# Last stage of a fused attention and two-mixture kernel: query tiles of 128, one shared last tile, later masks and another written order

## The chip, the cores and the metric

The kernel runs as one program on one core of a Trainium2 chip. The metric is the device time of one launch in microseconds; the time before is the median of three runs. A profiled execution of the same program gives the rows of this document; in it times count from the first instruction of the span.

## The reference

Three blocks follow one another, for 4 batches of 576 tokens and a width of 512. The last one is the one that the change touches:

```python
def _moe2_ref(x, w_gate, wq, wk, wv, wo):        # x: 4 x 576 x 512, 4 experts of width 64
    logits = x @ w_gate
    topk = np.argpartition(-logits, 2, axis=-1)[..., :2]
    ...                                          # w: softmax over the two chosen logits
    for e in range(E):
        q, k, v = x @ wq[e], x @ wk[e], x @ wv[e]
        scores = scale * (q @ k.transpose(0, 2, 1))
        scores = np.where(causal, -1000000000.0, scores)
        scores = scores - scores.max(-1, keepdims=True)
        a = np.exp(scores)
        a /= a.sum(-1, keepdims=True) + 1e-09
        ye = a @ v @ wo[e]
        ...                                      # out += (chosen weight of e, or 0) * ye
```

Before it stand a local attention plus an attention over pooled tokens (8 heads), and a mixer with a token part and a channel part of 1536 hidden channels. Everything is float32, and the products are made with more than one pass.

## The kernel before

The program has four stretches: the local and pooled attention with the token mixer (an order written out by hand, `STEPS`), the channel mixer (from about 180 us on, TensorE products of 460 and 462 columns, laid out by the scheduler), and then the last stage, the gated experts, whose order is the written table `LAST` (line 88). `tc.manual_schedule()` takes the words of the table one after the other, so that each engine's queue holds its own instructions in the order of the table; engines run freely against each other and wait by semaphores. Everything outside of those two tables is placed by the scheduler.

A word is a step and its indices. Per batch b: `vh`/`vl` split x into a high and a low part (ScalarE, GpSimd; two sets for six of the eight chunks of two batches, so batch 1 starts while batch 0 is in use), `v` makes values and gate logits of one token tile (12 products), `vc` and `lc` copy them out, `g`, `ge`, `gr`, `gw` make the gate weights. Per unit u = 2 b + p (batch b, expert pair p): `pj` projects half of the tokens to keys (0, 1) or queries (2, 3) with 12 products, `ph` and `pl` split the result into high and low parts, one expert's low part going to the other 64 partitions; `dk` swaps halves of K by DMA on SP's queue; `s.t.e` scores query tile t of expert e against all keys up to its end (two products, against K and its swapped copy; four for the last tile, in a PSUM tile of two banks of which there is one); `m` adds the causal mask and takes the row maximum (VectorE), `e` the exponential with its row sum (ScalarE), `q` the reciprocal, `r` the normalisation times the gate weight (VectorE), `t` turns the tile chunk by chunk on TensorE, `c` copies the turned chunks to SBUF (ScalarE), `a` multiplies by the values for one half of the queries (both experts side by side in the array), `ah`, `al` split the result. Per pair of batches: `w` multiplies 128 tokens by the output weights (3 products per expert pair), `y` copies the 512 columns out (in the last five tiles 288 by ScalarE and then 224 by VectorE), `dy` stores them.

Tokens go in tiles of TQ = 116: four of 116 and one of 112. For expert e of a unit the last tile is a 112 x 576 piece of its own with its own exponential, normalisation, five transposes and three copies. PSUM has six banks under the tag `b1`, given out in turn, and one tile of two banks. The score tiles (`Pc`) and output tiles (`y`) share eight SBUF buffers.

The masks `caus` (causal, line 173) and `before` (rank order of equal logits, line 174) are made by GpSimd at the head of the program, lines 187 to 193.

Of the kernel before, what the change touches and what calls it, by code (L numbers as in the profile page):

```python
# [13 lines left out]
OP = mybir.AluOpType  # L14
# [5 lines left out]
TQ = 116  # L20
NT = 5
TS = [TQ, TQ, TQ, TQ, S - 4 * TQ]
# [66 lines left out]
    vh0.0 vh0.1 vl0.0 vh0.2 vl0.1 vh0.3 vl0.2 vl0.3 v0.3 pj0.0 vh1.0 pj0.1 pj0.3 pj0.2 vh1.1 ph0.0 ph0.1 lc0.3 pl0.0  # L89
    ph0.3 v0.2 vc0.3 pl0.1 vc0.2 v0.0 lc0.2 lc0.0 dk0.0 ph0.2 pl0.3 pj1.0 dk0.1 s0.3.1 s0.3.0 pl0.2 s0.1.0 m0.3.1  # L90
    m0.3.0 s0.4.0 m0.4.0 ph1.0 pl1.0 e0.3.0 dk1.0 v0.4 e0.3.1 q0.3 vc0.0 s0.4.1 s0.0.1 m0.4.1 e0.4.0 lc0.4 s0.2.0
    v0.1 m0.2.0 pj1.1 e0.4.1 m0.1.0 vc0.1 vc0.4 s0.0.0 q0.4 lc0.1 g0 m0.0.1 vl1.0 gr0 m0.0.0 ge0 ph1.1 pl1.1 pj1.2
    dk1.1 vl1.1 e0.0.0 e0.1.0 pj1.3 gw0 ph1.2 e0.0.1 r0.3.0 r0.3.1 r0.4.0 t0.4.0 vh1.2 pl1.2 ph1.3 t0.3.0 t0.3.1
    s0.2.1 t0.5.0 pl1.3 s0.1.1 s1.4.0 r0.4.1 e0.2.0 vh1.3 m0.2.1 q0.0 c0.4.0 c0.3.0 m0.1.1 t0.4.1 c0.3.1 m1.4.0
    r0.0.1 c0.5.0 s1.3.0 vl1.2 e0.2.1 t0.5.1 m1.3.0 c0.4.1 vl1.3 q0.2 pj2.1 e0.1.1 ph2.1 t0.0.1 e1.3.0 q0.1 r0.0.0
    v1.0 r0.2.0 s1.3.1 r0.1.1 pl2.1 s1.4.1 vc1.0 lc1.0 r0.1.0 r0.2.1 c0.5.1 t0.2.0 s1.2.1 m1.3.1 e1.4.0 c0.0.1
    t0.1.0 c0.1.0 m1.4.1 m1.2.1 c0.2.0 v1.2 s1.2.0 e1.3.1 t0.0.0 dk2.1 e1.4.1 vc1.2 t0.1.1 pj2.0 c0.1.1 c0.0.0 q1.3
    m1.2.0 t0.2.1 e1.2.0 ph2.0 lc1.2 s1.1.0 s1.1.1 q1.4 r1.3.0 m1.1.0 r1.4.0 pj2.3 s1.0.1 pl2.0 m1.1.1 c0.2.1 t1.4.0
    ph2.3 r1.3.1 t1.5.0 m1.0.1 e1.1.0 t1.3.0 c1.3.0 e1.2.1 v1.4 c1.5.0 dk2.0 pl2.3 s1.0.0 lc1.4 q1.2 r1.4.1 e1.1.1
    r1.2.0 c1.4.0 v1.1 vc1.1 v1.3 t1.5.1 vc1.4 m1.0.0 t1.4.1 s2.3.0 q1.1 vh2.0 r1.1.0 c1.5.1 e1.0.0 r1.2.1 lc1.1  # L100
    lc1.3 e1.0.1 vc1.3 t1.3.1 m2.3.0 t1.2.1 c1.3.1 pj2.2 e2.3.0 c1.4.1 s2.3.1 s2.4.0 c1.2.1 g1 a0.1 q1.0 ge1 r1.1.1
    m2.4.0 a0.0 s2.4.1 t1.2.0 ph2.2 pl2.2 m2.3.1 t1.1.0 ah0.1 vh2.1 r1.0.0 ah0.0 al0.1 m2.4.1 al0.0 s2.1.0 e2.4.0
    m2.1.0 c1.1.0 r1.0.1 e2.3.1 t1.1.1 gr1 c1.1.1 c1.2.0 pj3.0 e2.1.0 ph3.0 t1.0.0 e2.4.1 pl3.0 s2.2.1 t1.0.1 s2.1.1
    c1.0.1 a1.1 m2.1.1 q2.3 c1.0.0 e2.1.1 m2.2.1 gw1 s2.2.0 pj3.1 q2.4 r2.3.0 ph3.1 ah1.1 pj3.2 r2.4.0 pj3.3 m2.2.0
    e2.2.0 pl3.1 al1.1 r2.3.1 e2.2.1 ph3.2 t2.4.0 ph3.3 r2.4.1 c2.4.0 t2.5.0 w0.3.0 q2.2 dk3.0 pl3.2 vh2.2 c2.5.0
    a1.0 q2.1 t2.5.1 vl2.0 pl3.3 w0.3.1 t2.3.0 vl2.1 ah1.0 t2.4.1 y0.3 c2.4.1 vl2.2 r2.2.0 c2.5.1 c2.3.0 r2.2.1
    w0.1.0 t2.3.1 al1.0 w0.1.1 s2.0.0 w0.2.0 r2.1.0 dk3.1 m2.0.0 y0.1 t2.2.1 vh2.3 w0.2.1 t2.2.0 s2.0.1 c2.3.1 y0.2
    t2.1.0 c2.2.0 s3.4.0 w0.0.0 c2.1.0 c2.2.1 e2.0.0 dy0.3 m2.0.1 e2.0.1 r2.1.1 s3.3.1 t2.1.1 vl2.3 dy0.1 q2.0
    m3.3.1 dy0.2 w0.0.1 s3.3.0 r2.0.0 y0.0 s3.2.0 s3.0.0 t2.0.0 m3.3.0 r2.0.1 m3.2.0 v2.0 vh3.0 e3.3.0 c2.1.1 m3.4.0
    t2.0.1 s3.2.1 s3.4.1 m3.0.0 e3.3.1 vc2.0 pj4.0 c2.0.1 pj4.1 q3.3 c2.0.0 m3.2.1 r3.3.0 ph4.0 lc2.0 e3.2.0 pl4.0  # L110
    v2.4 ph4.1 e3.4.0 e3.0.0 r3.3.1 t3.3.1 s3.0.1 t3.3.0 pl4.1 e3.2.1 c3.3.1 dy0.0 c3.3.0 m3.4.1 lc2.4 s3.1.0 dk4.0
    q3.2 r3.2.0 m3.1.0 pj4.3 vc2.4 a2.1 dk4.1 e3.4.1 vh3.1 ph4.3 m3.0.1 q3.4 s3.1.1 ah2.1 v2.2 a2.0 al2.1 r3.4.1
    pl4.3 r3.2.1 vc2.2 lc2.2 e3.1.0 ah2.0 t3.2.0 c3.2.0 s4.4.0 r3.4.0 t3.5.1 m3.1.1 t3.4.0 c3.4.0 m4.4.0 t3.5.0
    pj4.2 e3.1.1 vl3.0 c3.5.0 al2.0 s4.3.0 t3.2.1 c3.5.1 e3.0.1 ph4.2 q3.0 c3.2.1 v2.1 q3.1 vc2.1 pl4.2 s4.0.1
    r3.0.1 m4.3.0 r3.1.0 e4.4.0 vl3.1 v2.3 lc2.1 r3.0.0 t3.0.0 t3.4.1 t3.1.0 lc2.3 m4.0.1 g2 s4.4.1 vc2.3 t3.0.1
    c3.1.0 r3.1.1 m4.4.1 s4.1.0 c3.0.0 gr2 t3.1.1 s4.3.1 c3.4.1 s4.0.0 pj5.2 c3.0.1 ge2 m4.1.0 c3.1.1 e4.4.1 m4.0.0
    s4.2.0 q4.4 gw2 a3.1 r4.4.0 e4.0.0 e4.3.0 r4.4.1 m4.3.1 pj5.1 ph5.2 ah3.1 ph5.1 t4.4.0 pl5.2 c4.4.0 e4.0.1
    e4.3.1 al3.1 m4.2.0 pl5.1 t4.5.1 q4.3 pj5.3 t4.4.1 t4.5.0 a3.0 c4.5.0 pj5.0 dk5.1 r4.3.0 ph5.3 q4.0 c4.5.1
    r4.0.1 ah3.0 pl5.3 r4.0.0 e4.1.0 s4.2.1 c4.4.1 s4.1.1 vh3.2 ph5.0 t4.3.0 r4.3.1 al3.0 m4.2.1 pl5.0 vl3.2 m4.1.1
# [18 lines left out]
    c7.0.0 q7.1 t7.0.1 r7.1.0 r7.2.1 t7.5.1 w1.2.1 t7.4.1 c7.0.1 y1.1 r7.2.0 y1.2 c7.5.1 a6.0 r7.1.1 t7.2.0 ah6.0  # L138
    t7.2.1 dy1.1 al6.0 t7.1.1 c7.4.1 c7.1.1 w1.3.0 dy1.2 w1.7.0 t7.1.0 c7.2.0 c7.2.1 a7.1 w1.3.1 ah7.1 y1.3 w1.8.0
    w1.4.0 al7.1 c7.1.0 dy1.0 dy1.3 a7.0 w1.7.1 ah7.0 y1.7 w1.8.1 w1.6.0 al7.0 w1.4.1 dy1.7 w1.6.1 w1.5.0 y1.8 dy1.8  # L140
    y1.4 dy1.4 y1.6 w1.5.1 y1.5 dy1.6 dy1.5
"""


# [919 lines left out]
```

## Time and profile before

| | |
|---|---|
| time, median of 3 runs | 644.37 us (643.84 to 645.01) |
| profiled execution | 644.59 us, span 642.5 us |
| TensorE busy | 618.0 us, 96%, 5196 products |
| VectorE busy | 443.6 us, 69%, 1083 instructions |
| ScalarE busy | 361.5 us, 56%, 1061 instructions |
| GpSimd busy | 149.5 us, 23%, 167 instructions |
| mean granted TensorE clock | 0.999 |

A busy TensorE is a union of records, and records of successive products overlap: what a product takes from the queue is read from the starts of successive ones. In the groups by line a row has the number of instructions after the x, then busy time in us and the mean of one in ns. `PE` is TensorE, `PEld` its weight loads, `DVE` VectorE, `ACT` ScalarE, `POOL` GpSimd, `SPq` SP's queue of DMA issues; the text in brackets is idle time of the engine before the instruction and what ended it.

### The profile page before, as it was taken

The numbers are of one execution on the slowest core, as the hardware profiler recorded it, in microseconds if no ns is written. First come the engines' busy times: TensorE is split into PE (matmuls) and PEld (weight loads), VectorE is DVE, ScalarE is ACT, GpSimd is POOL, SyncE is SP. The second block draws the span as 40 slices with busy tenths as digits, with TensorE's granted clock in tenths as the row PEclk, the third lists the DMA queues.
The fourth block names the chain that finished last, engine by engine and source line by source line (L and its number), as shares of the span: only waits on it lengthen the run. The fifth ranks groups of instructions, "written<-read, shape, count | busy, mean of one in ns | idle before, by whom it ended". The sixth has DMA issues, their size and how long they took to land.

```text
span 642.5 us, 13638 instructions
## 1 busy us (share of the span) xinstructions
PE 618.0 (96%) x5196; PEld 554.6 (86%) x5196; DVE 443.6 (69%) x1083; ACT 361.5 (56%) x1061; POOL 149.5 (23%) x167
## 2 busy tenths in 40 slices
PE   4789999999999999999999999999989999999997
PEld 3678889999988889998888889999989889989885
DVE  7999998779696876467644554443497766857871
ACT  4898977765464453343422332420488777777783
POOL 6878986522131120010000000310010020010000
PEclk9999999999999999999999999999999999999999
DMA  8879484013132220020200100000111121021103
GB/s 266 250 234 279 130 248 119 13 46 116 42 106 88 66 87 12 1 66 0 67 0 1 51 16 1 2 0 1 44 35 37 29 76 38 20 100 40 37 33 117
DMA packets 28945, 46.76 MB, mean 73 GB/s; under 512 B 3216, under 2 KB 16016, under 8 KB 28880
## 3 DMA queue, kind: packets, MB, share of 16 engines
q1 hardware_dynamic: 28880, 45.90, 23.8%
q8 instruction: 41, 0.67, 0.5%
q14 instruction: 24, 0.20, 0.1%
HBM read 36.45 MB, written 4.72 MB: 64 GB/s over the span
## 4 chain that ended last, share of the span: by engine, by line
PE 87%; DVE 9%; DMA 1%; issue 1%; ACT 1%; POOL 1%; SPq 0%; ACTq 0%; DVEq 0%; POOLq 0%
PE c L219 47%; PE proj L219 7%; PE vp L219 4%; PE wo L219 4%; PE pu L219 4%; PE o L962 4%; PE pt L939 3%; PE h L219 3%; PE s L900 2%; PE s L901 2%; DMA wt_raw<-in_wt_dram 1%; PE tx L556 1%; PE sd L444 1%; DVE nraw L403 1%; PE tl L486 1%
## 5 line engine op out<-in xcount | busy, mean ns | idle before, releaser
L219 PE MATMUL c<-hl,wch 128*128 128x460 f32 (+1 forms) x240 | 89.3, 372 | 0.0
L219 PE MATMUL c<-hh,wcl 128*128 128x460 f32 (+1 forms) x240 | 89.1, 371 | 0.0
L219 PE MATMUL c<-hh,wch 128*128 128x460 f32 (+1 forms) x240 | 89.1, 371 | 0.0
L219 PE MATMUL c<-ul,wch 128*128 128x460 f32 (+1 forms) x240 | 89.0, 371 | 0.0
L219 PE MATMUL c<-uh,wch 128*128 128x460 f32 (+1 forms) x240 | 89.0, 371 | 0.0
L219 PE MATMUL c<-uh,wcl 128*128 128x460 f32 (+1 forms) x240 | 88.9, 370 | 0.0
L199 ACT ACTIVATE hh<-c 128x460 fp32r<-128x460 f32 (+1 forms) x60 | 33.0, 549 | 84.9 <-PE c L219 84.6
L795 POOL TENSOR_TENSOR vlo<-u,vh 128x576 fp32r<-128x576 f32 x16 | 22.8, 1427 | 238.7 <-ACT vh L791 215.1
L208 DVE SCALAR_TENSOR_TENSOR hl<-c,hh 128x460 fp32r<-128x460 f32 (+1 forms) x60 | 38.0, 634 | 48.7 <-ACT hh L199 48.5
L281 POOL TENSOR_TENSOR wc_t<-wc_f,wc_t 128x512 int32<-128x512 int32 x24 | 32.5, 1358 | 150.7 <-ACT wc_t L270 122.3
L663 DVE TENSOR_TENSOR ul<-u,uh 128x460 fp32r<-128x460 f32 (+1 forms) x80 | 53.1, 677 | 9.7 <-ACT uh L657 9.7
L657 ACT ACTIVATE uh<-u 128x460 fp32r<-128x460 f32 (+1 forms) x80 | 45.4, 585 | 23.8 <-PE c L219 19.0
L917 ACT ACTIVATE Pc<-Pc,nm 116x116 f32<-116x116 f32 (+4 forms) x80 | 46.7, 586 | 8.7 <-DVE nm L910 6.8
L910 DVE CUSTOM_DVE_ANT_0 Pc<-s,caus 116x348 f32<-116x348 f32 (+4 forms) x80 | 40.0, 514 | 14.6 <-PE s L901 10.9
L219 PEld LDWEIGHTS c<-hh,wch 128*128 128x128 f32 x240 | 45.2, 188 | 5.2
L219 PEld LDWEIGHTS c<-hh,wcl 128*128 128x128 f32 x240 | 45.1, 188 | 5.2
L219 PEld LDWEIGHTS c<-uh,wcl 128*128 128x128 f32 x240 | 45.1, 188 | 5.1
L219 PEld LDWEIGHTS c<-uh,wch 128*128 128x128 f32 x240 | 45.1, 188 | 5.0
L219 PEld LDWEIGHTS c<-hl,wch 128*128 128x128 f32 x240 | 45.1, 188 | 4.9
L219 PEld LDWEIGHTS c<-ul,wch 128*128 128x128 f32 x240 | 45.1, 188 | 4.9
L939 PE MATMUL pt<-ident,Pc 116*116 116x116 f32 (+2 forms) x240 | 35.2, 263 | 2.9 <-DVE Pc L928 2.6
L928 DVE TENSOR_SCALAR Pc<-Pc,su,gw 116x464 f32<-116x464 f32 (+4 forms) x80 | 36.3, 478 | 0.7
(216 smaller groups left out, 1650.6 us busy)
## 6 DMA issues: line engine op xcount, KB each, us to landing
wc_raw<-in_wc_dram SPq DMA_DIRECT2D x24, 512.0 KB, 3.6
vz<-in_vw_dram SPq DMA_DIRECT2D x16, 320.0 KB, 5.3
qT<-in_qT_dram SPq DMA_DIRECT2D x16, 288.0 KB, 5.0
kT<-in_kT_dram SPq DMA_DIRECT2D x16, 288.0 KB, 5.3
vr<-in_vp_dram SPq DMA_DIRECT2D x32, 144.0 KB, 4.2
K<-K SPq DMA_DIRECT2D x64, 72.0 KB, 2.0
out_dram<-y SPq DMA_DIRECT2D x18, 256.0 KB, 2.0
wt_raw<-in_wt_dram SPq DMA_DIRECT2D x4, 288.0 KB, 3.5
```

The source lines that it names most:

```text
L199: nc.scalar.activation(hi, src, AF.Relu if relu else AF.Copy, **({"scale": scale} if scale else {}))
L208: nc.vector.scalar_tensor_tensor(lo, src, 0.0, h, op0=OP.max, op1=OP.subtract)
L219: mm(ps, a, c, start=first and i == 0, stop=last and i == n - 1)
L281: nc.gpsimd.tensor_tensor(t, r["f"], t, op=OP.add)
L657: nc.scalar.activation(hi, UA[:, c, blocks[k]], AF.Copy)
L663: nc.vector.tensor_tensor(lo, UA[:, c, blocks[k]], hi.bitcast(F32), op=OP.subtract)
L795: nc.gpsimd.tensor_tensor(lo, U[b][:, c], hi.bitcast(F32), op=OP.subtract)
L910: nc.vector.tensor_tensor_reduce(dst, r["s", t, e], mask, -1.0, 3.0e38, OP.add, OP.min, nm[:nq])
L917: nc.scalar.activation(P[:nq, :n], P[:nq, :n], AF.Exp, bias=r["nm", t, e][:nq], scale=-1.0, accum_out=r["su", t][:nq, e:e + 1])
L928: nc.vector.tensor_scalar(P[:nq, :n], P[:nq, :n], r["su", t][:nq, e:e + 1], BR[b]["w"][:nq, t, 2 * p + e:2 * p + e + 1], op0=OP.mult, op1= ...
L939: tp(pt[:TS[c], (c - c0) * TQ:(c - c0) * TQ + nq], P[:nq, c * TQ:c * TQ + TS[c]], ident[:nq, :nq])
L962: mm(o[64 * e:64 * e + 64, a - q0:q1 - q0], BR[b]["VV"][:TS[c], c, ec:ec + 64], PT[e][:TS[c], column(c, a):column(c, a) + q1 - a], start=( ...
```

## The change

- `TQ` is 128: four query tiles of 128 and a rest `T4` of 64 tokens. The same tiles cut the keys and values into chunks of 128 and one of 64.
- The last tile holds 64 queries of expert 0 in partitions 0 to 63 and the same queries of expert 1 in partitions 64 to 127, in one of two fixed tiles `P4` of 640 columns, of which the last 64 are zero. Its scores and maxima are made per expert (`s.4.e`, `m.4.e`); exponential, reciprocal, normalisation, five 128 x 128 transposes and three copies are made once for both. The gate weights get a second small tile `gw4` for it, by two VectorE copies per batch. PT of both experts is one tile.
- Values `VV` and logits `L` get fixed tiles, whose rows 64 to 127 of the last token tile are zeroed once. GpSimd no longer clears L per batch.
- GpSimd fills `caus` and `before` and the zero parts behind the low parts of batch 0, just ahead of the last stage's table, not at the head of the program; `before` moves to another SBUF pool.
- The output tile that the table's last `w` makes (rows of batches 2 and 3, tile 5) is made in two halves of 256 columns, in two PSUM banks: VectorE copies the first and ScalarE the second, and each is stored by its own DMA.
- `LAST` is another table: the same steps in another order, without the second expert's `e`, `r`, `t` and `c` of the last tile.

```diff
-TQ = 116
+TQ = 128
 NT = 5
-TS = [TQ, TQ, TQ, TQ, S - 4 * TQ]
+T4 = S - 4 * TQ
+TROWS = [TQ, TQ, TQ, TQ, T4]
...
-    vh0.0 vh0.1 vl0.0 vh0.2 vl0.1 vh0.3 vl0.2 vl0.3 v0.3 pj0.0 vh1.0 pj0.1 pj0.3 pj0.2 vh1.1 ph0.0 ph0.1 lc0.3 pl0.0
-    ph0.3 v0.2 vc0.3 pl0.1 vc0.2 v0.0 lc0.2 lc0.0 dk0.0 ph0.2 pl0.3 pj1.0 dk0.1 s0.3.1 s0.3.0 pl0.2 s0.1.0 m0.3.1
-    m0.3.0 s0.4.0 m0.4.0 ph1.0 pl1.0 e0.3.0 dk1.0 v0.4 e0.3.1 q0.3 vc0.0 s0.4.1 s0.0.1 m0.4.1 e0.4.0 lc0.4 s0.2.0
-    v0.1 m0.2.0 pj1.1 e0.4.1 m0.1.0 vc0.1 vc0.4 s0.0.0 q0.4 lc0.1 g0 m0.0.1 vl1.0 gr0 m0.0.0 ge0 ph1.1 pl1.1 pj1.2
-    dk1.1 vl1.1 e0.0.0 e0.1.0 pj1.3 gw0 ph1.2 e0.0.1 r0.3.0 r0.3.1 r0.4.0 t0.4.0 vh1.2 pl1.2 ph1.3 t0.3.0 t0.3.1
...
-    w1.4.0 al7.1 c7.1.0 dy1.0 dy1.3 a7.0 w1.7.1 ah7.0 y1.7 w1.8.1 w1.6.0 al7.0 w1.4.1 dy1.7 w1.6.1 w1.5.0 y1.8 dy1.8
-    y1.4 dy1.4 y1.6 w1.5.1 y1.5 dy1.6 dy1.5
+    vh0.0 vl0.0 vh0.1 vh0.2 vl0.1 vl0.2 vh0.3 vl0.3 pj0.1 vh1.0 v0.1 pj1.1 vh1.1 v0.2 pj0.0 lc0.1 ph0.1 pl0.1 vl1.0
+    ph1.1 ph0.0 vc0.1 pl1.1 vc0.2 v0.0 pl0.0 pj0.3 pj1.0 ph1.0 lc0.0 lc0.2 pl1.0 ph0.3 pj0.2 ph0.2 vc0.0 v0.4 v0.3
+    pl0.2 dk0.1 lc0.4 pj1.2 dk0.0 pl0.3 vc0.4 lc0.3 s0.3.0 vc0.3 pj1.3 ph1.2 s0.3.1 s0.4.0 s0.1.1 vh1.2 g0 s0.1.0
+    gr0 vl1.1 m0.3.0 dk1.1 dk1.0 pl1.2 vl1.2 s0.2.0 ph1.3 s0.2.1 m0.3.1 m0.4.0 pl1.3 s0.4.1 vh1.3 m0.1.1 ge0 e0.3.0
+    s0.0.1 e0.3.1 s0.0.0 m0.1.0 m0.0.1 vh2.0 vl1.3 e0.1.0 m0.2.0 m0.2.1 gw0 q0.3 m0.4.1 s1.3.0 e0.1.1 v1.2 vc1.2
+    v1.0 e0.4 lc1.2 e0.2.0 pj2.1 e0.2.1 r0.3.0 ph2.1 lc1.0 r0.3.1 t0.3.0 vc1.0 s1.4.0 m0.0.0 pj2.0 q0.4 m1.3.0 q0.1
...
+    dy1.0 dy1.1 ah7.1 y1.3 al7.1 dy1.2 w1.8.0 dy1.3 w1.6.1 w1.7.1 w1.4.0 y1.6 y1.7 dy1.6 w1.8.1 dy1.7 y1.8 dy1.8
+    w1.4.1 w1.5.0 y1.4 w1.5.1 dy1.4 y1.5 dy1.5
...
+            r["w4"] = py.tile([TQ, 2], F32, tag="gw4", bufs=2, name="gw4")
+            for e in range(2):
+                es = slice(T4 * e, T4 * e + T4)
+                nc.vector.tensor_copy(r["w4"][es], r["w"][:T4, 4, e::2])
...
+            ps = b2("s")
+            r["s", t, e] = ps[:, :, :HS]
+            for h in range(2):
+                for i, K in enumerate((K1, K2)):
+                    mm(ps[:T4, h, :HS], Q[e][:, 4 * TQ:], K[e][:, h * HS:h * HS + HS], start=i == 0, stop=i == 1)
...
+            P, xs = P4[u % len(P4)], slice(T4 * e, T4 * e + T4)
+            r["P", t, None] = P
+            dst, mask = (y.rearrange("p (s n) -> p s n", s=2) for y in (P[xs, :S], caus[:T4, :S]))
+            nc.vector.tensor_tensor_reduce(dst, r["s", t, e][:T4], mask, -1.0, 3.0e38, OP.add, OP.min, nm[xs])
...
+        def turn(g, e=None):
+            t, cs = (g, range(g + 1)) if g < 4 else (4, range(4)) if g == 4 else (4, range(4, 5))
             pt = r["pt", g, e] = b1("pt")
+            for c in cs:
+                tp(pt[:, (c - cs[0]) * TQ:(c - cs[0]) * TQ + TQ], r["P", t, e][:, c * TQ:c * TQ + TQ], ident)
...
+            v = pt.rearrange("p (c e q) -> p e c q", e=2, q=T4)
+            if g == 4:
+                nc.scalar.activation(PT.rearrange("p e (c q) -> p e c q", q=S)[:, :, :, 4 * TQ:], v[:, :, :3], AF.Copy)
+            o = column(g - 1, 4 * TQ)
+            nc.scalar.activation(PT[:, :, o:o + T4], v[:, :, 3 if g == 4 else 0], AF.Copy)
...
     def project_out(g, t, p):
         if p == 0:
-            part[g, t] = b1("wo")
-        mm3(part[g, t], [(tuple(x[:, 128 * t:128 * t + 128] for x in OT[p]), WO[p])], first=p == 0, last=p == 1)
+            part[g, t] = [b1("wo") for _ in halves(g, t)]
+        for ps, cs in zip(part[g, t], halves(g, t)):
+            mm3(ps[:, :cs.stop - cs.start], [(tuple(x[:, 128 * t:128 * t + 128] for x in OT[p]), [x[:, cs] for x in WO[p]])],
+                first=p == 0, last=p == 1)
...
     for step, n in last:
         if step in ("vh", "vl") and n[0] == 0:
             BS[0][step](n[1])
+    nc.gpsimd.memset(caus, 0.0)
+    nc.gpsimd.affine_select(out=caus, in_=caus, compare_op=OP.is_ge, fill=-1.0e9, base=4 * TQ,
+                            pattern=[[-1, 5 * TQ]], channel_multiplier=1)
+    before = py.tile([128, E, E], F32, name="before")
...
+    for x in VVS + LS:
+        nc.gpsimd.memset(x[T4:, 4], 0.0)
+    for x in P4:
+        nc.gpsimd.memset(x[:, S:], 0.0)
```

## Rows read from the trace of the kernel before

**Rows 1.** Windows of the last stage: stretch, us, busy PE, PEld, DVE, ACT, POOL, clock.
```profile
449.30:471.98 22.68, 22.68 (x177) 22.54 (x175) 13.64 (x51) 11.72 (x33) 0.00 (x0) 1.00 0.21 47
471.98:478.20 6.22, 3.62 (x31) 3.15 (x30) 5.99 (x14) 5.15 (x16) 2.87 (x3) 1.00 0.11 25
478.20:600.00 121.80, 121.80 (x948) 110.37 (x947) 87.75 (x324) 91.38 (x287) 11.51 (x10) 1.00 0.16 45
600.00:638.54 38.54, 38.08 (x272) 30.20 (x271) 25.04 (x91) 26.17 (x86) 0.00 (x0) 1.00 0.18 59
```

**Rows 2.** Waits of PE in the last stage: us in total, times, longest.
```profile
PE pt L939 <- DVE Pc L928: 2.6, 1, 2.6
```

**Rows 3.** Timeline around 474 us: start us, us, engine and instruction.
```profile
472.10 2.62 DVE L928 TENSOR_SCALAR Pc<-Pc,su,gw 116x464 f32<-116x464 f32 x3
473.01 1.40 POOL L795 TENSOR_TENSOR vlo<-u,vh 128x576 fp32r<-128x576 f32 x1 [48.87 <-ACT vh L791]
...
474.87 1.36 PE L939 MATMUL pt<-ident,Pc 112*116 112x112 f32 x12 [2.60 <-DVE Pc L928]
...
476.67 0.58 DVE L928 TENSOR_SCALAR Pc<-Pc,su,gw 112x576 f32<-112x576 f32 x1
```

**Rows 4.** Timeline of PE: runs of transposes, of 128 columns and of 116.
```profile
36.40 0.38 PE L486 MATMUL tl<-ident,P 128*128 128x128 f32 x2
38.42 0.49 PE L486 MATMUL tl<-ident,P 128*128 128x128 f32 x3
...
625.97 0.56 PE L939 MATMUL pt<-ident,Pc 116*116 116x116 f32 x4
...
627.78 0.36 PE L939 MATMUL pt<-ident,Pc 116*116 116x116 f32 x2
```

**Rows 5.** Timeline of PE: successive score products.
```profile
461.54 0.37 PE L900 MATMUL s<-K,Q 128*116 128x464 f32 x1
461.75 0.37 PE L901 MATMUL s<-K,Q 128*116 128x464 f32 x1
...
465.23 0.28 PE L901 MATMUL s<-K,Q 128*116 128x256 f32 x1
465.35 0.32 PE L900 MATMUL s<-K,Q 128*116 128x348 f32 x1
465.51 0.32 PE L901 MATMUL s<-K,Q 128*116 128x348 f32 x1
```

**Rows 6.** Timeline of PE: attention times values, second and first half of the queries.
```profile
628.08 2.25 PE L962 MATMUL o<-PT,VV 116*64 116x288 f32 x20
...
632.56 1.10 PE L962 MATMUL o<-PT,VV 116*64 116x288 f32 x12
```

**Rows 7.** Timeline of the tail: last products, copies and issue.
```profile
638.08 0.39 PE L219 MATMUL wo<-wo_lo,oh 128*128 128x512 f32 x1
...
638.31 0.39 PE L219 MATMUL wo<-wo_hi,ol 128*128 128x512 f32 x1
638.78 0.41 ACT L989 ACTIVATE y<-wo 128x288 f32<-128x288 f32 x1 [1.01 <-PE wo L219]
639.23 0.39 DVE L991 COPY y<-wo 128x224 f32<-128x224 f32 x1 [1.03 <-ACT y L989]
...
639.65 0.33 SPq L995 DMA_DIRECT2D out_dram<-y  x1
```

**Rows 8.** The chain that ended last: start us, us of a value tile, a projection.
```profile
465.83 1.44 PE vp L219 x12
467.27 1.58 PE proj L219 x12
```

**Rows 9.** Groups by line of DVE in the last stage: count, busy us, mean ns, idle.
```profile
L212 DVE TENSOR_TENSOR K<-proj,K 64x288 fp32r<-64x288 f32 x32 | 14.6, 455 | 6.6 <-ACT K L199 5.6
...
L910 DVE CUSTOM_DVE_ANT_0 Pc<-s,caus 116x464 f32<-116x464 f32 x16 | 10.1, 635 | 3.6 <-PE s L901 3.5
```

**Rows 10.** Timeline of POOL at the head.
```profile
7.44 0.67 POOL L376 TENSOR_TENSOR pool<-kT 128x288 f32<-128x288 f32 x1 [1.55 <-DMA kT<-in_kT_dram]
```

## Prediction before the run

> **What bounds the kernel now.** I read the busy time by stretch first, for the last stage alone, because every edit but one small one lies in it. TensorE starts that stage at 449.3 us and gives its last product at 638.54 [rows 1, 7]. It is busy in all of the first 22.68 us, in 3.62 of the next 6.22, in all of the following 121.8 and in 38.08 of the last 38.54, at the full clock of 2.4 GHz throughout [rows 1]. So it idles for 2.60 + 0.46 = 3.06 us in 189.2; VectorE and ScalarE are each busy for some 70% beside it. The reader is to see a stage bound by TensorE's own queue, in which work taken from the other two engines gives nothing unless it ends one of TensorE's waits.
>
> The list of waits comes second. Its longest by far is 2.6 us of a transpose for a normalise [rows 2]. The timeline around it comes third. The first transposes of the stage wait until VectorE has done three normalises one after the other, 472.10 to 474.72, although one of the widest shape, 112 x 576, takes 0.58 us two microseconds after [rows 3]. What differs is that GpSimd subtracts a batch's low part (vl) beside it, 473.01 to 474.41, so of the 2.62 at least 2.62 - 3 x 0.58 = 0.9 us is the two engines in each other's way, about 1.
>
> **Transposes.** Per pair of experts and batch (eight of these "units") there were 2 x 15 transposes, 2 x 5 of them for the last query tile. Now both experts' last 64 queries share a tile, so there are 20 + 5: 240 become 200. A transpose's record is no price, since records overlap: a run of 2 of them takes 0.36 us and a run of 4 takes 0.56, so each costs 0.10 at 116 columns; 12 in 1.36 with the last tile's among them agree; with 128 columns, in an earlier stage, 2 take 0.38 and 3 take 0.49: 0.11 [rows 3, 4]. So 240 x 0.10 = 24.0 becomes 200 x 0.11 = 22.0: **-2.0 us**, give or take 1 for the view's steps of 0.01.
>
> **Scores.** Tiles 2 and 3 now score 384 and 512 keys where they scored 348 and 464. Starts of successive products lie 0.12 apart after 256 columns, 0.16 after 348, 0.21 after 464 and 0.23 after 512 [rows 5, 7]. By (0.16 - 0.12) / 92 a column costs 0.43 ns, so 384 takes 0.176. Each product grows by 0.016 and 0.02; two products (K1, K2) in each of two tiles for 16 experts give 2 x 0.036 x 16 = 1.15: **+1.2**. Tiles 0 and 1 ran 256 columns and still do; tile 4 still moves 2 x 288, only with 64 stationary columns in place of 112.
>
> **Attention times values.** The causal staircase gets finer to the right: the columns summed over key chunks were 288 + 172 + 56 for the first half and 3 x 288 + 228 + 112 for the second, and become 288 + 160 + 32 and 3 x 288 + 192 + 64: 1720 to 1600 per unit. The two groups that now take 2.25 and 1.10 us differ by 1204 - 516 = 688 columns, so a column costs 1.67 ns with both experts and both passes [rows 6]: 120 x 1.67 x 8 = **-1.6**. Value and query/key projections move the same columns as before and keep their time.
>
> **The order.** The new table puts 9 projections, 7 value tiles and 11 score steps ahead of the first transpose; the old one has 8, 5 and 8. With 1.58 and 1.44 for a projection and a value tile and the score prices above that is 28.4 us against 22.7 [rows 5, 8], so TensorE asks for its first normalise 5.7 us later, at 477.7. VectorE finishes it later too, by what the new order adds ahead of it: two low parts of a projection (4 x 0.455), two maxima (under 0.64 each), and three small copies (under 0.39 each), at most 4.3 us [rows 7, 9]. It had finished the first of the three at about 472.6, so now by 476.9, and it idled 9 of the first 22.7 us [rows 1, 3]. I leave 0.3 us of wait, and the other 0.46 as it is: **-2.3**. The bounds are -3.06 (no idle at all) and, if the new table has waits of its own, nothing or a loss (below). What is late next is VectorE again, since it is the one with the longest queue ahead of a transpose.
>
> **The tail.** Now the last product ends at 638.54, ScalarE copies 288 columns from 638.78, VectorE waits for it and copies 224 from 639.23, and SP issues the store at 639.65 [rows 7]. With the tile in two banks VectorE copies the first half while TensorE makes the second, and ScalarE alone copies the second: ready at about 638.78 + 0.41 = 639.19, not 639.62. The two stores queue on SP, which takes 0.33 for one, so the second is issued at about 639.35: **-0.3**. Bounds: -0.43 if SP never holds it up, +0.33 if a second store costs one issue more at the end. The six half products add 0.04.
>
> **What costs nothing.** The mask and the rank table are made later by GpSimd. At the start they delay only the first key pooling; the second, on which the first matmul of pooled scores waits, is held by its DMA until 7.44 [rows 10]. Bounds: 0 to -0.3. In the last stage they stand on GpSimd's queue ahead of batch 1's low parts; GpSimd does nothing in the first 22.7 us [rows 1], the mask's first reader runs 18.8 us into the stage, and batch 1's values first 24 us in. If that cover goes, because the fills wait for memory that the stage before still holds, up to four low parts of 1.4 us come late: +5 at most. VectorE: the merged tile saves 8 normalises of 0.58 and adds 8 small copies of gate weights (under 0.39 each) and wider tiles; nothing net. ScalarE loses 8 of 16 exponentials and 24 of its copies and gains 10% of width. Neither ends a wait of TensorE other than the one counted. Writing the second expert's rows to other partitions than they are read from is no new cost: the low part of K already crosses by 64 at 0.455 [rows 9]. The copy of 2 x 3 x 64 columns in one instruction is not shown; by the y copy of 288 it takes from 0.41 to twice that, and hides under ScalarE's 30% of idle time.
>
> **Sum.** -2.0 + 1.2 - 1.6 - 2.3 - 0.3 = **-5.0 us**. The profiled execution took 644.59 (its span of 642.5 and 2.1 around it), so 639.6; it lies 0.2 over the median of the runs, 644.37, which gives **639.4**.
>
> **Rivals.** *The idle time comes back.* The new table's waits add up to as much as the old one's 3.06 us; only the work and the tail change: -2.7, 641.7. For it: the order was written for durations that no wait on the chip honours exactly, as the 1 us beside GpSimd shows. Against it: in 160 us after its one long wait the old table idled 0.46. Chance 0.20.
>
> *Slower: normalises beside GpSimd.* The new order starts twelve low parts of 1.4 us in this stage, and the normalise that fell on one took some 1 us more than its 0.58 [rows 3]. Where that normalise is the one TensorE waits for, that reaches the end. The forecast has room for 5 of these; from 7 on it is slower by more than 1.3 us, and with 8 the time is 639.4 + 8 x 1.0 = 647.4. Against it: ten lay in this stage before, and one reached TensorE. Chance 0.05. The Trainium skill has it as a rule, in "GPSIMD Engine Reference", section "1. Specifications": GpSimd shares its SBUF interfaces with VectorE and contends with it where VectorE runs in a two-port mode or reads two SBUF inputs. By it a normalise beside any of the twelve would be slow, and with all of them on TensorE's path the time would be 639.4 + 12 = 651.4; the trace agrees on the one normalise and shows no such sum.
>
> *It does not do what it says.* The wider scores and transposes eat what the fewer transposes and columns save (transposes at their bound of -1.0, and new waits of 5 us, or the late fills above): 643.4 to 645.5. Chance 0.08.
>
> *More.* Besides the forecast all idle goes (-0.76) and the transposes gain 3 (-1.0): 637.6. Chance 0.06.
>
> *A transpose costs its latency.* The records last 0.26 us or more by the run of 2 that takes 0.36 [rows 4]; if TensorE could not overlap them, 40 fewer would give 240 x 0.26 - 200 x 0.27 = -8.4 in place of -2.0, and 633.0. The runs speak against it. The page "TensorE: Matmul & The Clock Gate", section "Part 4: PE-mode transpose", of the Trainium skill gives about 275 ns for one in a kernel, of which most is access latency; by it 40 fewer are worth 11 us, an estimate from that page. By the starts in this trace that figure is a record's length and not what the queue pays. Chance 0.02.
>
> **Numbers.** The forecast has 0.59 (its own range 638.0 to 641.0). Least of what a measurement of this kernel can tell is 0.2%, 1.3 us: faster is under 643.1. Forecast, idle back, more and latency make faster 0.86; same 0.08, slower 0.06. The range runs from 637.4 to 642.9 and holds the first, the second and most of "more".
>
> **What would show it.** 200 transposes where there were 240; 0.11 us between their starts; the pair of attention groups shorter by 0.2 us in all; TensorE's stretch from 449.3 to its last product about 184.5 us with idle under 1; no wait of 2 us for a normalise near 474; VectorE's copy of the last tile before TensorE's last product ends, and the last issue under 0.9 us after it. Wrong would be: idle of 2 us or more in TensorE's list of waits, a normalise of over 1 us there beside GpSimd, or a start of the last stage that isn't at 449.3.

## Result, and the profile after

The changed kernel takes **639.8 us** (median of 4 runs, 639.29 to 639.99) against 644.49 before (4 runs): a ratio of 0.9915, 95% interval 0.9897 to 0.9934. The forecast was 639.4 in a range of 637.4 to 642.9. The profiled execution took 639.29 us, its span 637.5.

The windows of the last stage of the changed kernel, from TensorE's first projection at 450.14 to 0.12 us (the pace of such products) after the start of the last one (stretch, us, busy PE, PEld, DVE, ACT, POOL, clock, DMA share, GB/s):

```profile
450.14:478.50 28.36, 28.31 (x214) 27.57 (x213) 16.77 (x59) 13.33 (x35) 4.67 (x7) 1.00 0.18 43
478.50:600.00 121.50, 121.50 (x933) 110.85 (x932) 94.91 (x352) 91.91 (x279) 10.03 (x7) 1.00 0.17 48
600.00:633.69 33.69, 33.69 (x244) 26.91 (x243) 20.12 (x70) 21.69 (x66) 0.00 (x0) 1.00 0.16 57
```

TensorE's stretch is 183.55 us with 0.05 idle, against 189.24 with 3.06 [rows 1]. Of the 5.7 us that the stage lost, 3.0 were idle time and 2.7 busy time. Its list of waits, with one row of 2.6 us before [rows 2], is empty.

The view hides one wait. Around 473.5 six score products and the load of their operands stand so:

```profile
473.27 1.61 PE L888 MATMUL s<-K,Q 128*128 128x256 f32 x6
...
473.62 0.30 PEld L888 LDWEIGHTS s<-K,Q 128*128 128x128 f32 x2 [0.16 <-DVE Q L198]
```

Four of them start 0.22 to 0.33 us apart, where such products (three of 256 columns, one of 512) elsewhere take 0.12 and 0.23: some 0.5 us of waiting, part of it for VectorE's low part of Q. It does not show as idle time, since the records overlap.

The place of the old wait, in the changed kernel's timeline (start us, us, engine and instruction), VectorE first, then TensorE:

```profile
478.48 0.54 DVE L926 TENSOR_SCALAR Pc<-Pc,su,gw 128x512 f32<-128x512 f32 x1
...
479.00 0.54 DVE L926 TENSOR_SCALAR Pc<-Pc,su,gw 128x512 f32<-128x512 f32 x1
```
```profile
479.07 0.30 PE L207 MATMUL proj<-vh,wk_lo 128*128 128x288 f32 x1
479.21 0.60 PE L932 MATMUL pt<-ident,Pc 128*128 128x128 f32 x4
479.56 0.78 PE L894 MATMUL s<-K,Q 128*64 128x288 f32 x4
...
615.40 1.07 PE L960 MATMUL o<-PT,v 128*64 128x288 f32 x12
...
625.27 2.12 PE L960 MATMUL o<-PT,v 128*64 128x288 f32 x20
```

The first normalise ends at 479.02 and the first transpose starts in its turn at 479.21: 0.2 us of slack in place of 2.6 of wait. Four transposes last 0.60 us where four of 116 columns lasted 0.56 [rows 4]; the two groups of attention times values are 0.16 us shorter together than 2.25 + 1.10 [rows 6].

The tail of the changed kernel [rows 7]:

```profile
633.53 0.42 DVE L1004 COPY y<-wo 128x256 f32<-128x256 f32 x1 [0.23 <-PE wo L207]
633.57 0.28 PE L207 MATMUL wo<-wo_hi,ol 128*128 128x256 f32 x1
633.93 0.38 ACT L1002 ACTIVATE y<-wo 128x256 f32<-128x256 f32 x1 [1.05 <-PE wo L207]
```

VectorE copies the first half while the second half's last product runs; the copies end at 634.31, 0.74 us after that product's start, where they ended 1.31 after it (639.62 - 638.31).

GpSimd's rows of the changed kernel, at the head and around the start of the last stage:

```profile
3.21 0.62 POOL L1015 MEMSET caus<- 128x640 f32 x1
3.90 0.24 POOL L181 TENSOR_SCALAR_AFFINE_SELECT band<-band 64x64 bf16<-64x64 bf16 x1
4.21 0.72 POOL L1016 TENSOR_SCALAR_AFFINE_SELECT caus<-caus 128x640 f32<-128x640 f32 x1
...
423.38 1.43 POOL L783 TENSOR_TENSOR vlo<-u,vh 128x576 fp32r<-128x576 f32 x1 [3.46 <-ACT vh L779]
449.09 0.12 POOL L1019 MEMSET before<- 128x16 f32 x1 [24.29 <-PE c L207]
449.27 0.56 POOL L1023 MEMSET v<- 64x256 f32 x2
...
470.41 1.43 POOL L783 TENSOR_TENSOR vlo<-u,vh 128x576 fp32r<-128x576 f32 x1 [19.80 <-ACT vh L779]
```

Two things are to be seen here. The causal mask, put later in the program, still runs at the head. And the rank table and the fills of the spare rows start only after 24 us of idle time that a product of the stage before ends (they wait for memory that it holds), but six low parts (the sixth at 423.38) had gone ahead of them. Run 9 shows what hangs on that.

### The profile page after: what moved, and what is told of

It is laid out like the page before. It is cut to its first block, busy times and chain, and to the rows that moved or that the text cites. A ratio compares the mean times of both kernels' runs of the same rounds, so it can differ in the third digit from the quotient of the medians.

```text
span 637.5 us, 13509 instructions
## 1 busy us (share of the span) xinstructions
PE 615.6 (97%) x5162; PEld 553.9 (87%) x5162; DVE 442.8 (69%) x1083; ACT 353.3 (55%) x1021; POOL 150.4 (24%) x169
## 4 chain that ended last, share of the span: by engine, by line
PE 90%; DVE 7%; DMA 1%; issue 1%; POOL 1%; SPq 0%; ACT 0%; ACTq 0%; POOLq 0%
PE c L207 47%; PE proj L207 8%; PE vp L207 5%; PE wo L207 4%; PE pu L207 4%; PE o L960 4%; PE pt L932 4%; PE s L888 3%; PE h L207 3%; PE s L894 1%; DMA wt_raw<-in_wt_dram 1%; PE tx L544 1%; PE sd L432 1%; DVE nraw L391 1%; PE olx L519 1%; PE tl L474 1%
## 5 line engine op out<-in xcount | busy, mean ns | idle before, releaser
L187 ACT ACTIVATE hh<-c 128x460 fp32r<-128x460 f32 (+1 forms) x60 | 32.9, 548 | 85.8 <-PE c L207 85.4
L915 ACT ACTIVATE Pc<-Pc,nm 128x512 f32<-128x512 f32 (+3 forms) x64 | 35.6, 560 | 2.6 <-DVE nm L903 2.2
L680 DVE TENSOR_TENSOR acc<-c,acc 128x460 f32<-128x460 f32 (+1 forms) x40 | 25.3, 635 | 16.4 <-PE c L207 15.4
L903 DVE CUSTOM_DVE_ANT_0 Pc<-s,caus 128x512 f32<-128x512 f32 (+3 forms) x64 | 30.0, 486 | 6.7 <-PE s L888 5.9
L939 ACT ACTIVATE PT<-pt 128x384 f32<-128x384 f32 (+2 forms) x64 | 25.3, 411 | 13.1 <-PE pt L932 12.3
```

What stands on the lines that cost most here:

```text
L187: nc.scalar.activation(hi, src, AF.Relu if relu else AF.Copy, **({"scale": scale} if scale else {}))
L680: nc.vector.tensor_tensor(dst[:, c, sl], cs_["s", g, k, c][:, :NB[k]], src[:, c, sl], op=OP.add)
L903: nc.vector.tensor_tensor_reduce(P[:, :n], r["s", t, e], caus[:, 4 * TQ - d0:5 * TQ], -1.0, 3.0e38, OP.add, OP.min, nm)
L915: nc.scalar.activation(P[:, :n], P[:, :n], AF.Exp, bias=r["nm", t, e], scale=-1.0, accum_out=r["su", t][:, x:x + 1])
L939: nc.scalar.activation(PT[:, e].rearrange("p (c q) -> p c q", q=S)[:, :m, g * TQ:g * TQ + TQ], pt[:, :m * TQ].rearrange("p (c q) -> p c q" ...
```

## Experiments

Ratios are to the kernel before on the same chip, with their 95% intervals. The kernel before took 645.86 us beside runs 1 to 3, 645.58 beside runs 4 to 7, 646.34 beside runs 8 to 10 and 646.24 beside runs 11 and 12.

**Run 1: the new tiles in the old order.** The table is the old one; of the two words of each last tile (e0.4.0 and e0.4.1, and so for r, t and c) the later one stays.

```diff
-    r0.3.0 r0.3.1 r0.4.0 t0.4.0 vh1.2 pl1.2 ph1.3 t0.3.0 t0.3.1 s0.2.1 t0.5.0 pl1.3 s0.1.1 s1.4.0 r0.4.1
+    r0.3.0 r0.3.1 vh1.2 pl1.2 ph1.3 t0.3.0 t0.3.1 s0.2.1 pl1.3 s0.1.1 s1.4.0 r0.4
```

> The tiles of 128 and all other edits, but the table of before (its words for the second expert's last tile left out). Theory (tiles and order save separately): the TensorE work of the last stage stays at the 183.5 us of the changed kernel, and the waits of the old table come back, 2 to 3 us of idle, the first of them behind a normalise beside a GpSimd subtraction near 473 us: 642 to 643 us. Rival 1 (the tiles took the waits away, the order is worth nothing): 639.8, idle under 0.3. Rival 2 (all of the gain is the order's): 644.4, with work of 186.

643.39 us, ratio 0.9963 (0.9950 to 0.9975). TensorE's waits in the last stage (us in total, times, longest):

```profile
PE pt L931 <- DVE Pc L925: 1.6, 3, 1.0
PE pt L931 <- DVE p L925: 1.4, 1, 1.4
PE s L887 <- ACT PT L942: 0.6, 1, 0.6
```

VectorE's normalises ahead of the first and the second of these rows and GpSimd's subtraction beside the second, from the timelines:

```profile
474.63 1.00 DVE L925 TENSOR_SCALAR Pc<-Pc,su,gw 128x512 f32<-128x512 f32 x2
...
477.59 1.50 DVE L925 TENSOR_SCALAR p<-p,su,gw 128x576 f32<-128x576 f32 x1
...
477.36 1.41 POOL L782 TENSOR_TENSOR vlo<-u,vh 128x576 fp32r<-128x576 f32 x1 [0.46 <-ACT vh L778]
```

The tiles alone keep 2.4 us; 3.6 come back as waits, where 2 to 3 were expected, and again a normalise beside GpSimd takes 1.50 us. Both rivals fall: the order is worth something, and not all. The theory missed on one point: the first wait stands behind two normalises that took their usual 1.00 us together, and only the second behind one beside GpSimd.

**Run 2: the last 64 queries of each expert in a tile of their own.**

```diff
-            P, xs = P4[u % len(P4)], slice(T4 * e, T4 * e + T4)
+            P, xs = P4[2 * (u % 2) + e], slice(0, T4)
...
-                tp(pt[:, ...TQ], r["P", t, e][:, c * TQ:c * TQ + TQ], ident)
+                tp(pt[:TROWS[c], ...nq], r["P", t, e][:nq, c * TQ:c * TQ + TROWS[c]], ident[:nq, :nq])
-                    mm(..., BR[b]["VV"][:, c, ec:ec + 64], PT[:, e, ...])
+                    mm(..., BR[b]["VV"][:TROWS[c], c, ec:ec + 64], PT[:TROWS[c], e, ...])
```

> The changed kernel with the last 64 queries of each expert in a tile of their own (its own exp, normalise and ten transposes of 64 columns each in place of five of 128). Theory 1 (a transpose costs by its moving columns, 25 x 128 = 3200 a unit either way): TensorE work unchanged within 0.3 us, 639.8 us, and the gain of the transposes came from 128 in place of 116, not from the one tile. Theory 2 (each transpose has a price of its own of about 0.11 us, as the prediction multiplied it): 40 more of them, +4.4 us, 644.2. Either way 8 more normalises and 8 more exps of about 0.58 us on VectorE and ScalarE, which cost nothing if they are covered; idle of TensorE shows it if they are not.

647.32 us, ratio 1.0026 (1.0015 to 1.0036): 7.5 over the changed kernel and slower than before. Neither theory had it. TensorE's timeline, a block of ten such transposes and a group of 20 products of attention times values:

```profile
487.69 0.82 PE L933 MATMUL pt<-ident,p 64*128 64x64 f32 x10
488.44 0.62 PE L887 MATMUL s<-K,Q 128*128 128x384 f32 x2
...
507.78 2.26 PE L963 MATMUL o<-PT,v 128*64 128x288 f32 x20
```

Their starts lie 0.062 apart, so a transpose goes mostly by its moving columns (0.109 at 128), and by that price 80 against 40 cost only 0.6 us. But the group of 20 products, in which operands of 128 rows are followed by such of 64, takes 2.26 where it took 2.12; the groups of 12, all of 128 rows, take what they took. Around a block of 64-row transposes the starts are also longer, by some 0.25 us over that price in the median of the 15 blocks, most of it at the first transpose and at the product behind the last. Waits shown: 0.7 us.

**Run 5, to part them: the tiles apart, but 128 rows high with 64 zero** (the lines with a minus are run 2's).

```diff
-    P4 = [py.tile([T4, S], F32, name=f"p4{i}") for i in range(4)]
+    P4 = [py.tile([128, S + T4], F32, name=f"p4{i}") for i in range(4)]
-                tp(pt[:TROWS[c], ...nq], r["P", t, e][:nq, c * TQ:c * TQ + TROWS[c]], ident[:nq, :nq])
+                tp(pt[:, ...TQ], r["P", t, e][:, c * TQ:c * TQ + TQ], ident)
```

> The changed kernel with the last 64 queries of each expert in a tile of their own again, but each such tile is 128 rows high (64 of them zero) and its ten transposes and its products stay 128 rows by 128 columns. In the first try (64 rows high) the tiles apart cost 7.5 us, of which 80 transposes of 64 columns at 0.062 us against 40 of 128 at 0.109 explain 0.6. Theory 1 (TensorE loses about 0.1 to 0.2 us each time it goes from operands of 128 rows to such of 64 and back, seen as 174 ns in all sixteen places where the products change): no such change is left, so the cost is that of 40 more transposes, 40 x 0.109 = 4.4 us and less than 1 us of waits: 644.2 to 645. Theory 2 (the 7.5 us are waits for eight more normalises, exps and copies that the order has no room for): these are all still there, and the transposes cost 4.4 in place of 0.6: 650 to 651.

647.26 us, ratio 1.0025 (1.0009 to 1.0040), between the two theories. The products of attention take what they took in the changed kernel, so their loss was the change of rows. The transposes' starts add up to 6.8 us more: 40 x 0.109 = 4.4 for their number, and 2.4 in gaps at the starts of groups, with 0.6 more among the output products. So the extra normalises, exps and copies cost about 3 us in an order not made for them. In run 2 the change of rows is the largest part, an estimate from its starts: 8 x 0.15 us in attention and about 15 x 0.25 around the transposes, some 5 of its 7.5; the 64 columns of those transposes changed with their rows, so the two are not told apart there.

**Run 4: the old tiles in the new order.** The table is the new one, with two words for each of the merged tile. With the old tiles' eight shared buffers alone this order locks up, the engines waiting for one another in a circle; so the last tiles have four of their own here, and the row maxima eight in place of six.

```diff
-    q0.2 ph2.0 t0.3.1 r0.4 c0.3.1 c0.3.0
+    q0.2 ph2.0 t0.3.1 r0.4.0 r0.4.1 c0.3.1 c0.3.0
-            P = r["P", t, e] = py.tile([128, S], F32, tag="Pc", ...)
+            P = r["P", t, e] = py.tile([128, S], F32, tag="Pc", ...) if t < 4 else P4[2 * (u % 2) + e]
```

> The tiles of 116 and the code of before in the new order (each word of the merged tile written for both experts); the second expert's and first expert's last tiles get four score tiles of their own in place of the rotating ones, without which the new order locks up on the eight rotating ones. Run 1 of this study (the new tiles in the old order) lost 3.6 us to the changed kernel, all of it waits of TensorE. Theory (tiles and order save separately): work of TensorE stays at the 186.2 us of before, idle falls from 3.06 to under 0.5: about 3 us under the before of the same call. Rival (the new order fits only the new tiles: sixteen more normalises and forty more transposes come between): idle stays at 2 to 3 us, within 1 us of before.

644.50 us, ratio 0.9987 (0.9978 to 0.9997). TensorE's waits:

```profile
PE pt L938 <- ACT PT L946: 0.5, 1, 0.5
PE pt L938 <- DVE p L927: 0.4, 2, 0.2
PE vp L218 <- ACT PT L946: 0.2, 1, 0.2
PE proj L218 <- ACT PT L950: 0.2, 1, 0.2
```

The wait of 2.6 us is gone, but 1.3 us of others have come, behind the copies and normalises that the narrow tiles have more of. TensorE's busy time did not stay: it is 187.5 us where it was 186.2 before. The rival is nearer: alone, the order is worth 0.8 us here. Tiles alone 2.4, order alone 0.8, both together 6.1 beside run 1: the two don't add, since each alone leaves waits (3.6 and 1.3 us) that the two together don't show.

**Run 7: the kernel before, two splits later.**

```diff
-    r0.4.0 t0.4.0 vh1.2 pl1.2 ph1.3 t0.3.0
+    r0.4.0 t0.4.0 pl1.2 ph1.3 vh1.2 t0.3.0
-    r0.4.1 e0.2.0 vh1.3 m0.2.1 ... c0.3.1 m1.4.0
+    r0.4.1 e0.2.0 m0.2.1 ... c0.3.1 vh1.3 m1.4.0
```

> The kernel before, with only two words moved: the splits of value channels 1.2 and 1.3 into high parts stand later (behind the scores' splits and the first copies), so that GpSimd's subtraction for 1.2 does not run beside the normalise of the first last tile near 473 us. Theory (that normalise takes 1.76 us in place of 0.58 because of the subtraction beside it, and the longest wait of TensorE hangs on it): the normalise falls to about 0.6 us, the wait of 2.6 us to about 1.4, and the time by 1.0 to 1.2 us against the before of the same call. Rival (the wait hangs on the exp and the order ahead of the normalise, or another step is late instead): normalise shorter but the wait still above 2 us, time within 0.4 us.

643.93 us, ratio 0.9977 (0.9968 to 0.9985), 1.5 us. VectorE's three normalises, GpSimd's subtraction behind them, and TensorE's wait:

```profile
473.33 1.44 DVE L927 TENSOR_SCALAR Pc<-Pc,su,gw 116x464 f32<-116x464 f32 x3
...
475.22 1.43 POOL L794 TENSOR_TENSOR vlo<-u,vh 128x576 fp32r<-128x576 f32 x1 [49.84 <-ACT vh L790]
```
```profile
PE pt L938 <- DVE Pc L927: 1.4, 1, 1.4
```

With nothing beside them the three take 1.44 us, not 2.62 [rows 3], and the wait is 1.2 shorter. So 1.2 of the old 2.6 was GpSimd's doing: shown. The time fell by 1.5, somewhat more than the 1.0 to 1.2 expected; the surplus isn't explained.

**Run 8: the same two words moved in run 1's kernel.**

```diff
-    r0.3.0 r0.3.1 vh1.2 pl1.2 ph1.3 t0.3.0 ... e0.2.0 vh1.3 ... t0.4 c0.3.1
+    r0.3.0 r0.3.1 pl1.2 ph1.3 vh1.2 t0.3.0 ... e0.2.0 ... t0.4 c0.3.1 vh1.3
```

> The new tiles in the old order (run 1: 643.39 us, TensorE waiting 3.6 us, of which 1.4 for the merged tile's normalise that took 1.50 beside a subtraction of GpSimd) with the splits of value channels 1.2 and 1.3 placed later as in run 7. Theory (slow normalises beside GpSimd are part of what the new order avoids): that normalise takes 0.6, its wait falls by 0.9: 642.4 to 642.6 us, the other 2.2 us of waits stay. Rival (the old order's waits hang on its sequence alone): 643.4.

643.98 us, ratio 0.9965 (0.9952 to 0.9978): run 1's ratio, so nothing gained. VectorE's and GpSimd's timelines:

```profile
476.89 0.58 DVE L925 TENSOR_SCALAR p<-p,su,gw 128x576 f32<-128x576 f32 x1
...
477.99 1.34 DVE L918 TENSOR_SCALAR su<-su 128x2 f32<-128x2 f32 x1
...
477.87 1.43 POOL L782 TENSOR_TENSOR vlo<-u,vh 128x576 fp32r<-128x576 f32 x1 [0.95 <-ACT vh L778]
```

The merged tile's normalise takes 0.58 and its wait falls from 1.4 to 0.5, as expected. But the later subtraction now meets an addition of two columns, normally 0.17 us, which takes 1.34, and the waits for the next normalises rise from 1.6 to 2.4. The stall moved on to the next instruction; the time of the theory was wrong.

**Run 6: each transpose twice.**

```diff
-            for c in cs:
+            for c in [c for c in cs for _ in range(2)]:
```

> The changed kernel with each transpose done twice into the same place (200 more). Theory (a transpose costs its place in TensorE's queue, 0.109 us from start to start in the changed kernel's trace): +21.8 us, 661.6. Rival (it costs the 0.27 us that its row shows, start to end): +54, 694. A third (most lie in stretches where TensorE would wait anyway): under +15.

661.56 us, ratio 1.0251 (1.0229 to 1.0273): 21.8 us over the changed kernel, 0.109 each. The latency rival, 0.27 each, is out by 32 us, and the third, under 15, by 7.

**Run 3: the last output tile whole.**

```diff
-        return [slice(0, DM // 2), slice(DM // 2, DM)] if [g, t] == end else [slice(0, DM)]
+        return [slice(0, DM)]
```

> The changed kernel with the last output tile whole, as before (three products of 512 columns, one bank, copies by ScalarE and VectorE after the last product, one DMA). Theory (the tail is 0.15 us shorter by the two profiles, 3.81 against 3.96 us): +0.15 us, 639.9 to 640.0. Rival 1 (as the prediction had it): +0.3. Rival 2 (the end is set by the DMA's landing alone): 0.

639.78 us, ratio 0.9910 (0.9892 to 0.9927): the changed kernel's own time. What the halves save is too small to measure.

**Runs 9 and 10: mask and rank table at the head; the changed kernel again.**

```diff
+    nc.gpsimd.memset(caus, 0.0)
+    nc.gpsimd.affine_select(out=caus, ...)
+    nc.gpsimd.memset(before, 0.0)
+    nc.gpsimd.affine_select(out=before, ...)
     UA = cst.tile([128, NP, B * S], F32, name="u")
...
-    nc.gpsimd.memset(caus, 0.0)
-    nc.gpsimd.affine_select(out=caus, ...)
-    before = py.tile([128, E, E], F32, name="before")
-    nc.gpsimd.memset(before, 0.0)
-    nc.gpsimd.affine_select(out=before, ...)
     for x in VVS + LS:
```

> The changed kernel with the causal mask and the rank table made at the head, as before. Theory (as the prediction had it, nothing waits for them): 0, within 0.3 us of the changed kernel in the same call. Rival (they stand before the channel loads' masks and delay the first poolings): up to +0.5 us, all of it ahead of 15 us.

> The changed kernel itself, beside the others of this call. Its first result was 4.7 us under before (639.8 against 644.49): the same again if that is not a matter of the chip it ran on, with the last stage on TensorE at 183.5 us and its start scattering between 449.3 and 451.2 as in the runs so far.

The changed kernel again took 639.82 us, ratio 0.990 (0.9883 to 0.9918). With mask and table at the head it took 644.89, ratio 0.9980 (0.9967 to 0.9992): 5.1 us lost, and not at the head. GpSimd's timeline and TensorE's waits:

```profile
435.36 0.31 POOL L1024 MEMSET v<- 64x256 f32 x1 [125.46 <-PE c L215]
...
449.80 0.31 POOL L1026 MEMSET p<- 128x64 f32 x2 [9.52 <-PE c L215]
450.05 8.26 POOL L791 TENSOR_TENSOR vlo<-u,vh 128x576 fp32r<-128x576 f32 x6
```
```profile
PE proj L215 <- POOL vlo L791: 1.9, 4, 0.7
```

and its windows, the clock in the third column from the end:

```profile
449.00:452.00 3.00, 2.74 (x15) 2.19 (x13) 1.27 (x2) 0.00 (x0) 2.20 (x4) 1.00 0.00 0
452.00:456.00 4.00, 2.32 (x9) 1.54 (x8) 0.00 (x0) 0.00 (x0) 4.00 (x4) 0.77 0.00 0
456.00:460.00 4.00, 4.00 (x19) 4.00 (x19) 0.82 (x3) 0.81 (x2) 2.32 (x2) 0.50 0.08 18
460.00:464.00 4.00, 4.00 (x30) 4.00 (x29) 1.16 (x3) 0.81 (x2) 0.00 (x0) 0.88 0.23 55
```

In this build the fills stand ahead of every low part, GpSimd waits with them, and six low parts run from 450.05 on, when TensorE wants four of them at once. It waits 1.9 us in four pieces; in the midst of them its clock falls to 0.50, the level of 1.2 GHz, and stays there until 461. Both theories were wrong in where they looked; this is the late fill that the prediction had priced at "+5 at most". The number fits by luck: the price was for low parts that come late, and some 3 us of the loss in this profile is the clock (454.2 to 461.0, busy for 6.5 us at half speed), of which it says nothing.

**Run 11: mask and table at the head, the fills behind five low parts.**

```diff
-    for x in VVS + LS:
-        nc.gpsimd.memset(x[T4:, 4], 0.0)
-    for x in P4:
-        nc.gpsimd.memset(x[:, S:], 0.0)
     with tc.manual_schedule():
         for step, n in last:
+            if (step, n) == ("ph", [1, 2]):
+                for x in VVS + LS:
+                    nc.gpsimd.memset(x[T4:, 4], 0.0)
+                for x in P4:
+                    nc.gpsimd.memset(x[:, S:], 0.0)
```

> Run 9 (mask and rank table at the head) took 644.9 us, 5.1 more than the changed kernel: there the fills of the value, logit and score tiles' spare rows stand ahead of all low parts in GpSimd's queue, wait for memory of the stage before until 449.8, and six low parts run behind them from 450.05 to 458.3; TensorE waits 1.9 us for four of them and then runs at 1.2 GHz until 461. Here the mask and table stay at the head and only the fills move, behind five of the low parts. Theory (all of the 5.1 is the fills' place): 639.6 to 640.2. Rival (part of it is the mask at the head): above 641.

639.96 us, ratio 0.9904 (0.9888 to 0.9920). All of the 5.1 us was the fills' place. Where mask and table stand costs nothing by itself.

**Run 12: the kernel before again, one execution with its profile.**

> The kernel before once more, for its profile alone: beside the other runs it took 644.1 to 648.4, with mean clocks of 0.991 to 1.0, the slower the lower, while the changed kernel stayed within 639.45 and 640.07. Theory (after the wait of 2.6 us near 474 the clock falls to 1.2 GHz in some executions): if this profile's clock is 0.996 or less, its rows after 475 us show the lower level. Rival (the low clock lies elsewhere, at the head where both kernels have it): it shows before 30 us.

647.57 us at a mean clock of 0.994, 3.0 more than the first profile; 2.7 of these lie in the last stage. Its windows and TensorE's transposes behind the wait:

```profile
449.00:471.00 22.00, 22.00 (x170) 21.80 (x169) 12.53 (x46) 10.47 (x29) 0.00 (x0) 1.00 0.20 44
471.00:475.00 4.00, 1.60 (x13) 1.37 (x11) 3.79 (x9) 3.89 (x12) 1.40 (x1) 0.95 0.26 61
475.00:480.00 5.00, 4.81 (x23) 4.74 (x24) 3.62 (x13) 3.16 (x10) 1.47 (x2) 0.50 0.00 0
480.00:484.00 4.00, 4.00 (x28) 3.75 (x27) 2.97 (x12) 1.84 (x6) 0.00 (x0) 0.82 0.00 0
```
```profile
475.19 2.52 PE L939 MATMUL pt<-ident,Pc 112*116 112x112 f32 x12 [2.58 <-DVE Pc L928]
```

After the same wait of 2.58 us the clock is at 1.2 GHz for some 6 us; the twelve transposes take 2.52 us where they took 1.36 [rows 3]. In the first profile the same wait left the clock at 1.00. So the wait cost 2.7 us beyond itself in this execution and nothing in the first. This can be part of why the kernel before ranges over 644.1 to 648.4 beside these runs and the changed one over 639.48 to 640.00 (run 10), with a gap of 6.5 us there and of 4.7 in the first comparison. It is not shown for the other executions, and it can't be all: six of them at a mean clock of 1.0 took 644.4 to 646.2. Nor does a low mean clock say where it fell. The profiles of runs 1, 2, 6 and 7 have the lower level between 29 and 39 us, the rival's place or near it, and not in the last stage; run 7's, at a mean of 0.995:

```profile
28.00:34.00 6.00, 4.89 (x112) 4.46 (x112) 5.83 (x18) 5.50 (x23) 4.08 (x6) 0.58 0.80 232
```

## Why the prediction was right, point by point

To compare works by kind, the time from each product's start to the next was added up by the tile written, over TensorE's rows of the last stage (before: 449.30 on, 189.0 us to the last start; after: 450.14 on, 183.4):

| us | before | after | change | forecast |
|---|---|---|---|---|
| transposes, without waits | 20.6 | 17.9 | -2.7 | -2.0 |
| scores | 31.0 | 32.9 | +1.9 | +1.2 |
| attention times values | 25.6 | 24.3 | -1.3 | -1.6 |
| projections, values, output | 108.0 | 108.3 | +0.3 | 0 |
| gaps in which it waited | 3.8 | 0.0 | -3.8 | -2.3 |

A record runs on for some 0.17 us past the start of the next product in a full queue, so a gap between starts is that much longer than the idle time in it; hence 3.8 here for the 3.06 of the view, of which the forecast was made.

- **The sum** of -5.0 is what the two profiled spans show (642.5 and 637.5), and in part by luck: the stage's stretch lost 5.7 where -4.7 was forecast, its later start took 0.8 back, and the tail gave 0.15 in place of 0.3. In runs 3, 10 and 11 the changed kernel, or one that differs from it in a detail that costs nothing, lies 6.1 to 6.5 us under the kernel before; what makes that more than here is open, but for what run 12 shows.
- **Transposes and scores** come to -0.8 together, as forecast, but each alone is 0.7 off. Their sums hang on what stands beside them: the last transpose of a group gives way after 0.03 us, and the score product that follows pays what it left (0.20 in place of 0.12); ahead of attention it pays 0.20 itself, in seven places before and in four after. And 0.5 of the scores' +1.9 is the hidden wait near 473.5, so the agreement of the two is partly chance. The price of 0.11 us is confirmed by run 6, at 0.109. Why 200 cost less than 240 was put too simply: run 2 shows the price going by columns, and the columns are 20 x 116 + 10 x 112 = 3440 a unit before and 25 x 128 = 3200 after, which 64-query tiles apart would also have. What the one tile saves beside 64-row tiles are the changes of rows and the eight normalises, exps and their copies (runs 2 and 5).
- **The Trainium skill's figure** for a transpose in a kernel ("TensorE: Matmul & The Clock Gate", section "Part 4: PE-mode transpose", about 275 ns, mostly access latency) is what a row lasts here. In the groups by line of the changed kernel (count, busy us, mean ns of one, idle):

```profile
L932 PE MATMUL pt<-ident,Pc 128*128 128x128 f32 x160 | 26.6, 273 | 0.0
```

  The queue paid 109 ns (run 6), so the measurement decides against 275 as a price.
- **Attention times values** was mis-sized by 0.3. The last product of a group of 12 takes 0.15 us to the next product, with 56 columns as with 32, so its share of the saving is not there; and two groups that ran on without a break before (32 products from 499.21) no longer do.
- **The order**: the forecast left 0.76 of the view's 3.06 us idle; 0.05 was left, and the 0.5 that the view hides. What it called late next, VectorE, was late by nothing, but by a margin of 0.2 us and not of the 0.8 that it worked out. VectorE's first normalise ended 28.9 us into the stage, where at most 27.6 was forecast, and TensorE asked for it at 29.1 and not at 28.4, held up by the hidden wait itself. The bound on VectorE failed; that no longer wait came of it is partly luck.
- **The tail** shrank by 0.15 in the profile, from 3.96 to 3.81 us after TensorE's end; run 3 can't tell it from nothing. The forecast of 0.3 went by the last issue, which did come 0.4 earlier behind TensorE's end (634.41 against 633.69, and 639.65 against 638.54); from there to the end it took 3.1 us in place of 2.9, which the forecast held equal.
- **The start of the stage** was to stay at 449.3 and came at 450.14, one of the prediction's own signs of being wrong. Twelve other profiles have it from 449.6 to 451.2, in kernels whose earlier stages hardly differ, the two of the kernel before being the earliest. What makes these 0.8 us is left open; they hid what the terms above had won beyond the forecast.
- **What costs nothing** was right on the time, and for another reason than given in part: the mask never left the head, and the cover of the fills was the six low parts that happened to be ahead of them. Run 9 is the same change without that cover, and lands at 644.9, in the range of the rival in which it "does not do what it says".
- **Slower: normalises beside GpSimd**: run 7 confirms the mechanism and its size (1.2 us). It reached no wait after the change: ten low parts and not twelve lie in the stage, three normalises started beside one, and only one of them took longer than usual, 0.91 us for 0.47 (at 536.42), with TensorE busy.
- **The chances** of forecast, idle back, more and latency add up to 0.87, and slower has 0.05; the 0.86 and 0.06 under Numbers are slips and change nothing.

## What to carry to other kernels

An engine that is bound by its own queue is served by an order only together with the tiles it was made for: take the sum of two such edits from one plan, not from each alone. Before costing a fill or a mask at nothing, look at what stands behind it in its engine's queue and which memory it waits for; the build may put it elsewhere than the program does. And a wait in a busy TensorE can cost its length again in clock: 2.6 us of it cost 2.7 more in one execution here and nothing in another.

## What was not expected of the hardware

- VectorE's normalises and additions from SBUF that started well before the end of a subtraction of 128 x 576 by GpSimd were over only 0.02 to 0.32 us behind that end: 1.76 us for 0.58 before, 1.50 in run 1, and 1.34 for 0.17 on two columns in run 8. Not every instruction is held: the low parts of Q, which read PSUM too, took their usual 0.47 beside it (four in 1.90 us in run 8, at 474.96), and a reciprocal of two columns its usual 0.17 (at 552.73 in the changed kernel).
- TensorE's clock fell to 1.2 GHz after one wait of 2.58 us (run 12) and in the midst of four waits of 1.9 us together (run 9); after the same wait of 2.60 us in the first profile it stayed.
- Going from operands of 128 rows to such of 64 cost TensorE about 0.15 us in each of the eight groups of products of run 2 that do so (1.2 us in all; the expectation of run 5 has 174 ns and sixteen places, which is miscounted: the step itself is 0.256 us where it is 0.156 in the changed kernel), and some 0.25 around each of its 15 blocks of 64-row transposes. Between 116 and 112 rows none is seen.
